# Sharing exponentials between ScalarE and VectorE: banks placed tile by tile, and two long passes in halves

## The chip, the cores and the metric

One core of a Trainium2 chip runs the whole program. The metric is device time of one execution in microseconds, lower is better. A core has five engines with a queue each: TensorE (PE, matmuls), ScalarE (ACT, activation functions), VectorE (DVE, element-wise work), GpSimd (POOL) and SyncE (SP, which here only issues DMAs). The queues run in order, and engines wait for one another by semaphores. PSUM, where matmuls write, has 8 banks of 512 float32 columns in each of 128 partitions.

## The reference

Four attention blocks with a residual, on 2048 tokens of width 640, 32 heads of width 20. Layers 0 and 2 look at a window of 256 keys, layers 1 and 3 at all keys.

```python
def _B_ref(x, wqkv, wo):            # layers 1 and 3; _A_ref (0 and 2) adds the window's mask
    qkv = (x @ wqkv).reshape(B, S, 3, H, Dh).transpose(2, 0, 3, 1, 4)
    q, k, v = qkv[0], qkv[1], qkv[2]
    scores = jnp.einsum("bhqd,bhkd->bhqk", q, k) * (Dh ** -0.5)
    p = _softmax(scores, axis=-1)
    o = jnp.einsum("bhqk,bhkd->bhqd", p, v)
    return o.transpose(0, 2, 1, 3).reshape(B, S, D) @ wo

x = x + _A_ref(_layernorm(x), A_wqkv, A_wo)
x = x + _B_ref(_layernorm(x), B_wqkv, B_wo)
x = x + _A_ref(_layernorm(x), A_wqkv, A_wo)
x = x + _B_ref(_layernorm(x), B_wqkv, B_wo)
```

## The kernel before

**Units, banks, tiles.** The kernel is one Python function that writes all queues by hand. Queries go in 4 chunks `c` of 512, heads in 8 groups `g` of four. A `Unit` is one layer, chunk and head group. Its work is a list of *banks*: for one block of 128 keys (`kc`, 16 of them) and one head `j`, the scores of 128 keys by 512 queries, which fill one PSUM bank; a full layer's unit has 64. Units stand in one list, `units`: layer 0, with parts of layer 1 chunk 0 woven in; the rest of layer 1 chunk 0; layer 1 chunks 1 to 3, with the window units of layer 2 between; layer 3 chunk 0 in two parts (key blocks 0 to 11, then 12 to 15), with layer 2's last chunk; layer 3 chunks 1 to 3. The main loop takes one *tile* per turn (a *tick*), as a rule three banks: three score matmuls into PSUM banks 0 to 2 or 3 to 5 by turns (L1359), one exponential by ScalarE over all three (L1387, 1536 columns to a bf16 tile `pt`), and some ticks later the matmuls with the values (L1420), which add into bank 7 (`op`).

**Background.** Projections, normalisations, transposes, output projections and the `tails` that end a unit are generators. `pump` and `keep_clock` run pieces of them between tiles; `keep_clock` also puts in matmuls that nobody reads (`unread`, or "owed" ones ahead of the next scores) when the tick has had too little TensorE work. Background results use PSUM bank 6 (`take_m`, `drop_m`), and VectorE empties it (L331, L579, L1128). All by-columns matmuls carry the line of their helper, L307.

**VectorE's exponentials.** Some banks of layers 1 and 3 are not given to ScalarE. VectorE computes their exponential in fixed point, for two banks at a time: a pass for each bank from PSUM to int32 (`side_fixed`, L957, 512 columns), then a chain over 1024 columns (`t_chain`): the fraction (L969) and its square (L978), the cubic (L980), and the whole part put in as the exponent (L982). The values matmuls of these banks are in `side_values` (L1010). Which banks they are is fixed when a `Unit` is made (`put_aside`): the last four (layer 1, chunks 1 to 3), the last six or eight in turn (layer 3 from chunk 1 group 1 on; four in the very last unit). None come from layer 1 chunk 0, layer 3 chunk 0 or the unit (3,1,0).

**Where they run.** Up to the final chunks (layer 3, chunks 1 to 3) the tiles are planned in a list ahead of the loop: a unit that gives banks gives them to its own tiles, 5 tiles apart, and such a tile has two banks for ScalarE (1024 columns) and one for VectorE, which reads it in place. In the final chunks tiles are full, and VectorE's score goes by itself into bank 6 (`side_scores`, L944), when the planner's count of VectorE's backlog, `state["lag"]`, is below `LAG` and no background piece holds the bank. The count rises with each VectorE instruction that is emitted (0.7 for a short pass, 1.2 for a long one) and falls by a tile's ScalarE time. `side_work` emits steps of the chain while it is below `WORK`, at the end of each tick. Working buffers: in layer 1 the float32 tile `raw_o`; from layer 3 chunk 1 on three tiles of `xnT`, with results in unused parts of `ka` and `qa` (`side_start`).

**Queues.** SP issues a unit's loads of queries, keys and values (L798, L810, L812) as soon as one of three key buffers is free; POOL issues the stores of projections and the loads of weights, and masks window banks (L1463).

Of the kernel before, what the change touches and what calls it, by code (L numbers as in the profile page):

```python
# [25 lines left out]
G = 8  # L26
# [14 lines left out]
WORK = 1.0  # L41
SIDE_1 = 4
SIDE_3 = (6, 8)
# [9 lines left out]
def kernel(  # L53
# [272 lines left out]
    def evac(out_, in_):  # L326
        if state["act"]:
            nc.scalar.copy(out=out_, in_=in_)
        else:
            state["lag"] += 0.6  # L330
            nc.vector.tensor_copy(out=out_, in_=in_)  # L331
# [60 lines left out]
    def stats(l, c, i):  # L392
        if (l, c) not in mvs:
            mvs[l, c] = lnp.tile([P, 4, 2], F32, name="mv", tag="mv")
        state["lag"] += 1.2
        st = lnp.tile([P, 2, 6], F32, name="stats", tag="stats")
        xv = x_sb[:, 4 * c + i, :]
        nc.vector.bn_stats(out=st[:, 0, :], in_=xv[:, 0:HD])
        nc.vector.bn_stats(out=st[:, 1, :], in_=xv[:, HD:D])
        nc.vector.bn_aggr(out=mvs[l, c][:, i, :], in_=st[:])  # L400
# [282 lines left out]
    def put_aside(l, c, g):  # L683

        if l == 1:
            n = SIDE_1
        else:
            n = 4 if (c, g) == (NC - 1, G - 1) else SIDE_3[g % 2]
        if n == 2:
            return ((NT - 1, 2), (NT - 1, 3))  # L690
        return tuple((NT - 1 - i // 4, i % 4) for i in range(n))

# [3 lines left out]
    class Unit:  # L696
        def __init__(self, l, c, g, part=None):
            self.l, self.c, self.g, self.part = l, c, g, part
            self.windowed = l % 2 == 0
            self.aside = ()  # L700
            if self.windowed:
                sets = [(m, b0, subs, j) for m, b0, subs in window_banks(c) for j in range(4)]
            else:

                if c > 0 and (l, c, g) != (3, 1, 0):
                    self.aside = put_aside(l, c, g)
                k0, k1 = key_blocks(l, part)
                sets = [
                    (None, 0, [(kc, 0, 4, 0)], j) for kc in range(k0, k1) for j in range(4)
                    if (kc, j) not in self.aside  # L710
                ]
            n = len(sets)
            self.banks = [
                (self, j, m, b0, subs, i < 4, i >= n - 4 + len(self.aside), i == n - 1)
                for i, (m, b0, subs, j) in enumerate(sets)
            ]
# [144 lines left out]
    def finish_unit(u):  # L861
# [31 lines left out]
    side_todo = deque(  # L893
        (u, p, i) for u in units for p in range(len(u.aside) // 2) for i in range(2)
    )
    side_left = Counter({id(u): len(u.aside) for u in units})
    side_out = {}
    side = {"xi": deque(), "chain": deque(), "out": deque(), "late": False}
# [7 lines left out]
    def side_start():  # L906

        assert live["xnT"] == 0 and not side["chain"] 
# [18 lines left out]
    def side_free():  # L927

        if not side_todo or not side["late"]:
            return False  # L930
        u, p, i = side_todo[0]
        return (
            id(u) in loaded and state["tick"] >= loaded[id(u)] + 8
            and mfree[6][0] <= state["tick"] and (i == 1 or len(side["xi"]) > 0)
        )

    def side_scores():

        u, p, i = side_todo[0]
        mseq[0] += 1  # L940
        mfree[6] = (state["tick"] + 2, mseq[0])
        kc, j = u.aside[2 * p + i]
# [4 lines left out]
    def side_fixed(z):  # L947

        u, p, i = side_todo.popleft()
        side_left[id(u)] -= 1  # L950
        if not side_left[id(u)] and id(u) in deferred:
            live["kt"] -= 1
            live["qt"] -= 1
        if i == 0:
            side["now"] = side["xi"].popleft()
        xi = side["now"]
        nc.vector.tensor_scalar(  # L957
# [4 lines left out]
        if i == 1:  # L962
            side["chain"].append(t_chain(u, xi))

    def t_chain(u, xi):

        V = nc.vector
        t = side["t"]
        V.tensor_scalar(  # L969
            out=t, in0=xi.bitcast(I16)[:, 0::2], scalar1=T1, scalar2=T0, op0=ALU.mult, op1=ALU.add  # L970
        )
        yield 0.7
        while not side["out"]:
            yield 0.0
        pt = side["out"].popleft()
        po = pt.rearrange("p a b -> p (a b)")
        q = po.bitcast(F16)
        V.tensor_tensor(out=q, in0=t, in1=t, op=ALU.mult)  # L978
        yield 0.7
        V.scalar_tensor_tensor(out=q, in0=q, scalar=TB, in1=t, op0=ALU.add, op1=ALU.mult)  # L980
        yield 1.2
        V.scalar_tensor_tensor(  # L982
            out=po.bitcast(U16), in0=xi.bitcast(I32), scalar=1.0 / C, in1=q,
            op0=ALU.mult, op1=ALU.add,
        )
        side["xi"].append(xi)
        side_out.setdefault(id(u), []).append((pt, state["tick"]))
        yield 1.2

    def side_work(force):  # L990

        while (force or state["lag"] < WORK) and side["chain"]:
            cost = next(side["chain"][0], None)
            if cost is None:
                side["chain"].popleft()
                continue
            if cost == 0.0:
                return False
# [5 lines left out]
    def side_values(u, pairs, done):  # L1004

        for n in range(done, len(pairs)):
            pt = pairs[n][0]
            for i in range(2):
                kc, j = u.aside[2 * n + i]
                nc.tensor.matmul(  # L1010
                    op[32 * j : 32 * j + VW, :], lhsT=u.v(kc, j), rhs=pt[:, i, :], start=False,
                    stop=all(jj != j for _, jj in u.aside[2 * n + i + 1 :]),
                    skip_group_check=True,
                )
            side["out"].append(pt)

    def side_push():
# [3 lines left out]
        if side_free():  # L1021
            side_scores()
            return
# [6 lines left out]
    def side_done(u):  # L1030

        n = 0
        while len(side_out.get(id(u), ())) < len(u.aside) // 2:
            n += 1
            assert n < 10000
            side_push()
        return side_out.pop(id(u))
# [5 lines left out]

    def s_emitted(u):
# [6 lines left out]
        elif side_left[id(u)]:  # L1051
# [187 lines left out]
    with tc.manual_schedule():  # L1239
# [11 lines left out]
        banks = [b for u in units for b in u.banks]  # L1251
        tiles = []
        starts = {}
        n = 0
        last_layer = sum(len(u.banks) for u in units[: index[3, 1, 0, None]])
        placed = {}
        while n < last_layer:
            size = 2 if len(tiles) % 2 and narrow(banks[n][0]) else 3
            u = banks[n][0]
            at = placed.setdefault(id(u), [])  # L1260
            extra = []
            if (
                len(at) < len(u.aside) and banks[n + 1][0] is u
                and len(tiles) >= (15 // (SIDE_1 - 1) if SIDE_1 > 2 else 3) * len(at) + (at or [0])[0]
            ):
                kc, j = u.aside[len(at)]
                extra = [(u, j, "side", 0, [(kc, 0, 4, 0)], False, False, False)]
                at.append(len(tiles))
                size = 2
            for b in banks[n : n + size]:  # L1270
                starts.setdefault(id(b[0]), len(tiles))
            tiles.append(banks[n : n + size] + extra)
            n += size
        for m, b in enumerate(banks[n:]):
            starts.setdefault(id(b[0]), len(tiles) + m // 3)
        banks = deque(banks[n:])

        side_now = False

        def next_tile(t):  # L1280

            if t < len(tiles):
                return tiles[t]
            size = 3
            if side_now:
                return [banks.popleft() for _ in range(min(size, len(banks)))]
            if t % 2 and not tails and state["held"] is None and mfree[6][0] < state["tick"]:
                if all(task.wake > state["tick"] for task in todo) :
                    size = 4
            return [banks.popleft() for _ in range(min(size, len(banks)))]  # L1290

        def rate(t):

            if t >= len(tiles):
                return 0.45
            u = tiles[t][0][0]
            if index[u.l, u.c, u.g, u.part] < woven:
                return 1.2
            done, r = 0.0, 0.6 if state["early"] else 0.3
            for task in todo:  # L1300
                done += max(task.left, 0.0)
                if task.need < len(units):
                    r = max(r, done / max(starts[id(units[task.need])] - t - 16, 1))
# [10 lines left out]
        last_tick[0] = len(tiles)  # L1314
# [4 lines left out]
        valued = 0  # L1319
# [4 lines left out]
        while ended is None or t < ended + 8:  # L1324
# [3 lines left out]
            if t < len(tiles) or banks:  # L1328
                if t >= len(tiles) and not side["late"] and not live["xnT"] and not todo:
                    side_start()  # L1330
                side_now = (
                    state["held"] is None and state["lag"] < LAG and side_free()
                )
                cur = next_tile(t)
# [28 lines left out]
                if cur[-1][2] == "side":  # L1363
                    cur = cur[:-1]
                    n_b -= 1
                    if "early" not in side:
                        side_early()
                    while not side_todo[0][2] and not side["xi"]:
                        assert side_work(True)
                    side_fixed(sp[:, n_b, :])  # L1370
                if side_now:
                    side_scores()
# [28 lines left out]
            for n in range(2 if n_b == 0 or t > closed + 1 else 0):  # L1401
# [15 lines left out]
                for m, (kc, q0, qn, col) in enumerate(subs):  # L1417
                    for _, pg, i, b in group:
# [4 lines left out]
                            start=(first and m == 0), stop=(last and m == len(subs) - 1),  # L1423
                            skip_group_check=u.windowed or len(u.aside) > 0,
                        )
                if first:
                    valued = 0
# [95 lines left out]
```

## Time and profile before

| | us |
|---|---|
| runs of the kernel (three): median, lowest, highest | 2191.64, 2187.83, 2196.76 |
| the profiled execution | 2197.81 |
| its span | 2196.1 |

The profiled execution falls into these stretches. A stretch begins with the first exponential of its first unit.

| stretch | us from the span's start | banks on VectorE |
|---|---|---|
| layer 0, with layer 1 chunk 0 woven in | 16 to 441 | 0 |
| layer 1 chunk 0, last key blocks | 441 to 497 | 0 |
| layer 1 chunk 1, with layer 2 | 497 to 753 | 32 |
| layer 1 chunk 2, with layer 2 | 753 to 1018 | 32 |
| layer 1 chunk 3, with layer 2 | 1018 to 1284 | 32 |
| layer 3 chunk 0, first part, with layer 2 | 1284 to 1500 | 0 |
| layer 3 chunk 0, second part | 1500 to 1558 | 0 |
| layer 3 chunks 1, 2, 3 | 1558 to 2182 | 56, 55, 47 |

How to read the lines: the page's busy line gives each engine's time, its share of the span and its instructions. A group of instructions has line, engine, operation, output and input with sizes, a count, then busy time in all and the mean of one in ns, then the engine's idle time just before them and what ended it. A line of waits says which engine at which line waited for which, how long in all in us, how often, and the longest. A line of stretches gives for each engine its busy time and instructions, then the granted clock of TensorE and the use of the DMA engines. Records of ScalarE's passes overlap their neighbours, so the distance between starts, not the mean length, is what a pass takes.

### The profile page before, as it was taken

Reading aid. Unit: us, or ns where it says so; the run is one execution under the profiler, and the core shown is the slowest. Engines: PE = TensorE matmul, PEld = TensorE weight load, DVE = VectorE, ACT = ScalarE, POOL = GpSimd, SP = SyncE. Lnnn points to the kernel's source line nnn. Section 1 sums busy time; section 2 is a strip of 40 time slices with the busy share of each in tenths; the row PEclk is TensorE's granted clock in tenths of the full one; section 3 lists DMA queues with packets and bytes.
Section 4 is the critical chain, followed back from the end, with each engine's and each line's share of the span. In section 5 each row is a group of like instructions: output and inputs, shape, how many; then the busy total and the mean of one; then the engine's idle time right before and its main releaser. Section 6 shows DMA issues by size and latency. Waiting matters only on the chain. (4 is left out here: it accounts for less than half of the span.)

```text
span 2196.1 us, 73000 instructions
## 1 busy us (share of the span) xinstructions
PE 1931.1 (88%) x31782; PEld 760.4 (35%) x31783; DVE 1324.3 (60%) x2308; ACT 2112.9 (96%) x1726; POOL 483.3 (22%) x952
## 2 busy tenths in 40 slices
PE   8999998988889888888888988888888988888887
PEld 3444443433333333333333433342222222222222
DVE  5556565425656666566665743532487778778873
ACT  7789899999999999999999999999999999999997
POOL 6665556110121113401143112511000000000000
PEclk9899999999999999999999999999999999999999
DMA  6223233322210323112231123122112111111100
GB/s 201 74 82 107 68 98 99 81 78 64 74 46 27 83 60 90 39 37 64 64 101 34 35 86 98 39 57 65 48 43 61 32 32 41 35 32 35 53 20 17
DMA packets 88416, 137.27 MB, mean 63 GB/s; under 512 B 20766, under 2 KB 63486, under 8 KB 88094
## 3 DMA queue, kind: packets, MB, share of 16 engines
q1 hardware_dynamic: 68878, 79.43, 13.1%
q0 software_dynamic: 19216, 53.17, 8.2%
q8 instruction: 249, 4.08, 0.8%
q14 instruction: 73, 0.60, 0.1%
HBM read 99.52 MB, written 27.79 MB: 58 GB/s over the span
## 5 line engine op out<-in xcount | busy, mean ns | idle before, releaser
L1387 ACT ACTIVATE pt<-ps 128x1536 bf16<-128x1536 f32 (+2 forms) x1646 | 2072.1, 1438 | 46.1 <-PE ps L1359 36.1
L1359 PE MATMUL ps<-qt,kt 32*128 32x512 bf16 x3938 | 542.4, 384 | 79.3 <-ACT pt L1387 70.2
L307 PE MATMUL ps<-masks,ident 128*32 128x512 bf16 x5676 | 504.6, 387 | 99.4 <-ACT pt L1387 54.8
L1420 PE MATMUL ps<-pt,vt 128*21 128x512 bf16 x3826 | 383.1, 387 | 1.1 <-issue 1.1
L1359 PEld LDWEIGHTS <-kt 32*128 32x128 bf16 x3938 | 161.0, 91 | 482.7 <-issue 461.0
L307 PEld LDWEIGHTS <-ident 128*32 128x32 bf16 x5676 | 179.9, 94 | 283.1 <-issue 254.7
L1463 POOL TENSOR_SCALAR_AFFINE_SELECT pt<-pt 128x256 bf16<-128x256 bf16 (+2 forms) x505 | 213.2, 444 | 184.4 <-ACT pt L1387 181.8
L307 PE MATMUL ps<-xnT,wqk 128*32 128x512 bf16 x3320 | 224.8, 381 | 12.4 <-DVE on L1128 2.8
L331 DVE CAST st<-ps 128x512 bf16<-128x512 f32 x134 | 92.7, 691 | 169.1 <-PE ps L307 164.9
L1420 PEld LDWEIGHTS <-vt 128*21 128x21 bf16 x3842 | 95.0, 89 | 254.9 <-issue 251.5
L957 DVE TENSOR_SCALAR xnT<-ps 128x512 int32<-128x512 f32 x158 | 109.2, 691 | 109.2 <-PE ps L944 108.4
L307 PE MATMUL ps<-wop,on 128*32 128x320 bf16 x3712 | 160.9, 300 | 6.8 <-DVE x_sb L579 3.3
L1474 DVE TENSOR_TENSOR pt<-pt,masks 128x512 bf16<-128x512 bf16 (+4 forms) x267 | 111.3, 433 | 61.3 <-ACT pt L1387 59.8
L307 PEld LDWEIGHTS <-on 128*32 128x32 bf16 x5760 | 122.2, 95 | 66.6 <-issue 33.6
L1359 PE MATMUL ps<-qa,ka 32*128 32x384 bf16 (+2 forms) x1408 | 114.5, 278 | 24.4 <-ACT pt L1387 21.2
L307 PE MATMUL ps<-wv,xnT 128*32 128x320 bf16 x2560 | 116.6, 302 | 7.9 <-DVE on L1128 3.3
L579 DVE TENSOR_TENSOR x_sb<-x_sb,ps 128x320 bf16<-128x320 bf16 x120 | 58.3, 486 | 105.8 <-PE ps L307 104.9
L307 PEld LDWEIGHTS <-wqk 128*32 128x32 bf16 x3320 | 83.5, 96 | 95.9 <-issue 38.0
L1128 DVE TENSOR_TENSOR on<-on,ps 128x512 bf16<-128x512 bf16 x128 | 86.3, 683 | 47.8 <-PE ps L307 46.9
L885 DVE CAST on<-ps 128x512 bf16<-128x512 f32 x112 | 77.1, 688 | 61.7 <-PE ps L1010 36.1
L957 DVE TENSOR_SCALAR raw_o<-ps 128x512 int32<-128x512 f32 x96 | 66.1, 689 | 61.4 <-PE ps L1359 60.3
L546 POOL DMA_DIRECT2D k_d<-st x75 | 42.6, 568 | 224.2 <-DVE st L331 209.1
(101 smaller groups left out, 1638.5 us busy)
## 6 DMA issues: line engine op xcount, KB each, us to landing
vt<-v_d SPq DMA_DIRECT2D x48, 336.0 KB
kt<-k_d SPq DMA_DIRECT2D x192, 80.0 KB
wqk<-in_B_wqkv_dram POOLq DMA_DIRECT2D x80, 160.0 KB, 3.5
wqk<-in_A_wqkv_dram POOLq DMA_DIRECT2D x70, 160.0 KB, 3.5
k_d<-st POOLq DMA_DIRECT2D x75, 128.0 KB, 2.3
q_d<-st POOLq DMA_DIRECT2D x75, 128.0 KB, 2.1
qt<-q_d SPq DMA_DIRECT2D x384, 20.0 KB
v_d<-vs POOLq DMA_DIRECT2D x16, 336.0 KB, 3.1
```

What stands on the lines that cost most here:

```text
L307: nc.tensor.matmul(out_[r], lhsT=lhsT[:, r], rhs=rhs, start=start, stop=stop)
L331: nc.vector.tensor_copy(out=out_, in_=in_)
L546: nc.gpsimd.dma_start(out=dst, in_=staging.pop())
L579: nc.vector.tensor_tensor(out=xv, in0=had, in1=yp, op=ALU.add)
L885: nc.vector.tensor_copy(out=oT, in_=op)
L957: nc.vector.tensor_scalar(out=xi.bitcast(I32)[:, i * C : (i + 1) * C], in0=z, scalar1=SCALE * LOG2E * FIX, scalar2=127.5 * FIX, op0=ALU.mu ...
L1128: nc.vector.tensor_tensor(out=oT, in0=oT, in1=zb, op=ALU.mult)
L1359: nc.tensor.matmul(sp[:, i, col * P : (col + qn) * P], lhsT=u.k(kc, j), rhs=u.q(j, q0, qn), start=True, stop=True,)
L1387: nc.scalar.activation(out=pt[:, i:k, b0 * P :], in_=sp[:, i:k, b0 * P :], func=ACT.Exp, scale=SCALE,)
L1420: nc.tensor.matmul(op[32 * j : 32 * j + VW, q0 * P : (q0 + qn) * P], lhsT=u.v(kc, j), rhs=pg[:, i, col * P : (col + qn) * P], start=(first ...
L1463: nc.gpsimd.affine_select(out=v, in_=v, compare_op=ALU.is_gt if later else ALU.is_ge, fill=0.0, base=0, pattern=[[0, k - i], [-1 if later ...
L1474: nc.vector.tensor_tensor(out=pt_[:, i:k, cols], in0=pt_[:, i:k, cols], in1=mv_, op=ALU.mult)
```

## The change

The list of tiles made ahead is gone, and each tile is made when its turn comes (`take`, `next_tile`). A unit keeps its banks in a queue, `rest`; tiles take from the front, and VectorE's banks are taken two at a time from the back (`side_take`), from a unit that `side_giver` finds: among the next three units whose loads were issued 8 ticks before, with at least 30 banks left in its queue (or 12 after its first pair). It gives none while the backlog count is not below 0.5, no working buffer is free or, before the final chunks' buffers are set up, the last bank was less than five tiles ago. All units of layers 1 and 3 but those of layer 1 chunk 0 may give, layer 3 chunk 0 among them, whose buffers are now set up (`side_start`) during its fourth head group or later, once at most one `xnT` is live and no window unit is.

A step of the chain is now emitted if the count with the step's own cost stays under a limit (2.2 in layer 3, 1.4 in layer 1), where the old test was the count alone, under 1.0. In layer 1 the two long passes run as two halves of 512 columns each. `side_values` emits the values of all pairs that are ready. Costs in the planner's count change (evacuations 0.7 or 0.5, statistics 1.1).

```diff
-WORK = 1.0
-SIDE_1 = 4
-SIDE_3 = (6, 8)
+LAG_1 = 0.5
+WORK = 2.2
+WORK_1 = 1.4
+KEEP = 30
+HALF = True
+MOST_1 = 64
+GAP_1 = 5
...
-    def side_free():
...
+    def side_giver():
+
+        if not side["late"] and state["tick"] < side["last"] + GAP_1:
+            return None
+        if side["half"] is not None:
+            return side["half"][0]
+        if not side["xi"]:
+            return None
+        while side["at"] < len(givers) and not givers[side["at"]].rest:
+            side["at"] += 1
+        for n in range(side["at"], min(side["at"] + 3, len(givers))):
+            u = givers[n]
+            if id(u) not in loaded or state["tick"] < loaded[id(u)] + 8:
+                return None
+            if not side["late" if u.l == 3 else "early"]:
+                return None
+            if u.l == 1 and len(u.aside) >= MOST_1:
+                continue
+            if len(u.rest) >= (KEEP if len(u.rest) + len(u.aside) < u.size else 12):
+                side["at"] = n
+                return u
+        return None
...
+        every = (slice(0, 2 * C),)
+        halves = (slice(0, C), slice(C, 2 * C)) if HALF and u.l == 1 else every
+        cost = 0.7 if len(halves) == 2 else 1.25
+        steps = [(fraction, h, 0.7) for h in every] + [(square, h, 0.7) for h in every]
+        steps += [(cubic, h, cost) for h in halves] + [(whole, h, cost) for h in halves]
+        return deque(steps)
...
     def side_work(force):
...
-        while (force or state["lag"] < WORK) and side["chain"]:
-            cost = next(side["chain"][0], None)
...
+            if not force and state["lag"] + cost > (WORK if side["late"] else WORK_1):
+                return False
...
+                giver = side_giver() if state["lag"] < (LAG if side["late"] else LAG_1) else None
+                if giver is not None and state["unit"] >= final and (
+                    state["held"] is not None or mfree[6][0] > state["tick"]
+                ):
+                    giver = None
+                cur = next_tile(t, giver)
```

## The prediction

> **What bounds the kernel now.** I read the busy shares of the page first:
>
> ```profile
> PE 1931.1 (88%) x31782; PEld 760.4 (35%) x31783; DVE 1324.3 (60%) x2308; ACT 2112.9 (96%) x1726; POOL 483.3 (22%) x952
> ```
>
> ScalarE (ACT) is busy for 96% of the span, and nearly all of it is the exponential of L1387. Then the busy times of stretches cut at the stage borders: layer 1 chunk 2, layer 3 chunk 0 (its first key blocks), layer 3 chunks 1 to 3.
>
> ```profile
> core 0: us, PE busy (x) PEld busy (x) DVE busy (x) ACT busy (x) POOL busy (x), PEclk, DMA share, GB/s
> 753.00:1018.00 265.00, 231.00 (x3877) 95.04 (x3870) 166.76 (x292) 261.56 (x205) 62.49 (x119) 0.99 0.23 62
> 1284.00:1500.00 216.00, 187.53 (x3255) 78.95 (x3245) 81.02 (x172) 214.92 (x161) 63.34 (x118) 1.00 0.24 67
> 1558.00:2180.00 622.00, 550.45 (x7287) 172.46 (x7284) 461.20 (x607) 617.89 (x457) 0.00 (x0) 1.00 0.12 36
> ```
>
> ScalarE is busy 99% of each stretch, VectorE (DVE) 63%, 38% and 74%. So from 441 us on the end is set by the columns ScalarE must pass, and VectorE has room, most of it from 1284 to 1558 us, where it takes no banks today. Next the groups by line with shapes kept apart, from 753 to 1284 us:
>
> ```profile
> L1387 ACT ACTIVATE pt<-ps 128x1536 bf16<-128x1536 f32 x342 | 473.1, 1535 | 9.3 <-PE ps L1359 8.7
> L1387 ACT ACTIVATE pt<-ps 128x1024 bf16<-128x1024 f32 x64 | 71.2, 1113 | 0.0
> ```
>
> The 64 narrow passes are the tiles that gave a bank to VectorE. The means, 1.535 and 1.113 us, overlap the neighbouring passes, so I price by starts: in the timeline unhindered passes of 1536 columns start 1.331 us apart, of 1024 columns 0.904 us. **A bank is worth 0.427 us, a pass costs 0.05 us beside its columns.** What the starts take beyond these prices is lost time: 28.1 us in layer 1 chunks 1 to 3 (497 to 1284 us, 624 passes, 96 banks on VectorE), 4.1 us from 1284 to 1558 us (203 passes, none on VectorE), 13.6 us from there to the last pass (158 banks). The idle column shows less, since a pass's record covers some of its wait.
>
> The waits tell whose slack is left. TensorE's (PE) own, 1558 to 2180 us:
>
> ```profile
> PE ps L307 <- ACT pt L1387: 40.5, 108, 0.9
> PE ps L944 <- DVE on L1128: 6.8, 19, 0.7
> PE ps L944 <- DVE x_sb L579: 5.2, 18, 0.6
> PE ps L1359 <- ACT pt L1387: 4.4, 15, 0.6
> ```
>
> Mostly TensorE waits for ScalarE (about 47 us here with a row of 2.2; the same query gives 80 us from 497 to 1558 us), and some 13 us for VectorE to empty the bank at L944.
>
> **The banks.** The order of the changed program, built but not run, has 302 fixed-point passes of VectorE where the old one has 254. Per stage: layer 1 chunks 1 to 3, 32+32+32 become 36+38+38 (+16); layer 3 chunk 0, none becomes 16+8 (+24); layer 3 chunks 1 to 3, 56+55+47 become 57+57+52 (+8). ScalarE's exponentials fall from 1650 to 1645 and lose 24,576 columns, 48 banks. 48 x 0.427 + 5 x 0.05 = **20.7 us less on the engine that sets the end.**
>
> **What a bank costs beside that.** A tile that gives a bank leaves ScalarE after 0.904 us, while TensorE still has three score matmuls, the values and a background block to do. Before, such passes took 0.08, 0.12 and 0.14 us over 0.904 on average in chunks 1 to 3, so 0.11. Bounds for the 40 banks up to 1558 us: 0.05, about what the late tiles with a bank lose over those without, and 0.16, which is 28.1 us less the quiet stretch's rate (4.1 / 203 x 624 = 12.6) over 96 banks. I take 40 x 0.11 = **4.4 us** (2.0 to 6.4). The late 8 go at 13.6 / 158 = 0.086: **0.7 us** (0.4 to 1.0).
>
> **VectorE's work.** From the groups with shapes kept apart:
>
> ```profile
> L957 DVE TENSOR_SCALAR raw_o<-ps 128x512 int32<-128x512 f32 x96 | 66.1, 689 | 61.4 <-PE ps L1359 60.3
> L980 DVE SCALAR_TENSOR_TENSOR raw_o<-raw_o 128x1024 f16<-128x1024 f16 x48 | 58.5, 1220 | 0.9
> L982 DVE SCALAR_TENSOR_TENSOR raw_o<-raw_o 128x1024 uint16<-128x1024 int32 x48 | 58.6, 1221 | 0.9
> L969 DVE TENSOR_SCALAR raw_o<-raw_o 128x1024 f16<-128x1024 int16 x48 | 33.2, 691 | 0.8
> ```
>
> 48 banks add 48 x 0.69 and 24 chains of two short passes (0.69 each) and two long ones (1.22 each): 33 + 92 = 125 us. The halves of layer 1 turn 112 long passes into 224. Half of one lies between 0.61 (no fixed part) and 0.69 us (a 512-column pass like L957), so the halves add 0 to 18 us; I take the upper end, nearest in shape. [...] All this lies beside ScalarE: by stage VectorE goes from 62% to about 70% (493 + 61 of 787 us), 35% to 58% (96 + 62 of 274 us) and 74% to 78% (461 + 21 of 622 us). Had it no room, the 143 us would be in the end.
>
> What reaches the path is lateness. In layer 1 a pass started ahead of an evacuation blocks it for up to 0.69 us instead of 1.22, and a tile gives a bank only while the planner's backlog is under 0.5 us, where places were fixed before. Waits of TensorE on VectorE there are some 32 us in the same view of 497 to 1284 us, most of it under its waits for ScalarE. I take **0**, between a gain of 5 us (a sixth of those waits) and a loss of 2 (more, smaller passes). In layer 3 chunks 1 to 3 passes may start on a higher planned backlog (limit 1.0 before a step, now 2.2 after it; the same ceiling for a long pass, more often reached). The planner's own count at the end of a tile rises there from 0.25 to 0.42 us on average, as the two programs are built. Against VectorE's lateness in proportion, 13.6 x 0.7 = 9.5 us is the worst; 0 the best, as TensorE's 47 us of waits for ScalarE cover it. I take **1 us**, since the longest wait on VectorE at L944 is 0.7 us in 622.
>
> **TensorE, DMAs, the end.** The matmuls are the same but for 20 more warming ones; each bank's score and two value matmuls only move. TensorE has 127 us of waits for ScalarE to give, of which 20.7 go. SP and POOL issue as many DMAs as before (1482 and 958 instructions on their queues). One load comes nearer to its use: layer 3 chunk 0 group 3, second part, is issued 4 tiles ahead instead of 8, 5.3 us. Its nine issues took 1517.7 to 1521.1 us before, 3.4 us, and POOL's DMAs land 2.1 to 3.5 us after issue: 0.2 to 1.6 us late. I take **0.5 us** once; what is queued behind it is one tile of scores. At the end one background projection finishes a tile later, but the last two value matmuls of VectorE's banks come earlier: **0** (-0.5 to +1).
>
> **Sum:** -20.7 + 4.4 + 0.7 + 0 + 1 + 0.5 + 0 = -14.1 us on a span of 2196.1 us: 2182.0. That execution took 2197.81 us, 0.3% over the median of the runs, 2191.64. From the median: **2177.5 us**. The bounds add to -23.6 and +0.8: 2168 to 2192.
>
> **Rivals.**
>
> *TensorE becomes the bound in the narrow tiles.* The gain of 0.427 us needs TensorE to follow in 0.904 us. Of the old narrow tiles, 67 that shared their tick with a background block lost 0.153 us, 29 without one 0.016. If the blocks crowd (3 score, 4 value and 20 projection matmuls in one tick were seen at 1248 us, with 0.64 us lost), the 40 banks cost 0.3 us each: 12 instead of 4.4, time 2185. Against it: 127 us of slack.
>
> *VectorE's lateness falls.* If halves and placing by backlog remove 5 us of layer 1's loss and layer 3's growing backlog stays covered: about -21, 2171 or lower.
>
> *Slower: a long pass put ahead of a bank's fixed-point pass in layer 3 chunks 1 to 3.* TensorE's next background matmul or side score into bank 6 waits for VectorE, and the values and scores behind it in TensorE's queue wait too. Price of one collision: 1.22 us less the 0.38 us that TensorE has at a mean wait on ScalarE (40.5 / 108), 0.84 us. It decides from 17 collisions (14.1 / 0.84), one in ten of 166 banks. At one in three, 55 x 0.84 = 46 us: 2177.5 + 46 = 2224. For it: the higher limit. Against it: 37 waits of 0.3 us in the old run for 158 banks, none over 0.7, and no higher ceiling.
>
> That the change gives VectorE no more banks is excluded by the built order.
>
> **How the numbers follow.** Forecast (2171 to 2183) 0.63; lateness falls 0.10; TensorE bound 0.18; slower 0.09. Half a percent, 11 us, is about what a measurement of this kernel can tell from no change (its three runs spread over 9 us). Faster than 2180.7: the second case and most of the first, 0.68. Slower than 2202.6: 0.07 of the last case. The rest, 0.25, is the same. The range takes the bounds above and 2 us at the low end and 1 at the high for the spread of the runs: 2166 to 2193.
>
> **What would show it.** The ScalarE group of 1024 columns near x276 and that of 1536 near x1284; the stretch that was 1284 to 1558 us about 8 us shorter, the layer 1 chunks together some 5 us, the last stretch about 2 us; VectorE near 1467 us busy, with passes of 512 columns at 0.61 to 0.69 us from the two halved lines; lost time from 441 us on near 52 us, where it was 46. Wrong if narrow passes start over 1.2 us apart on average (TensorE bound), or if TensorE's waits on VectorE at the side scores exceed 25 us (backlog).

## The result, and the profile after

The changed kernel takes 2174.09 us (median of four runs, 2173.51 to 2177.99), the kernel before 2189.9 us beside it. The ratio is 0.992, 95% interval 0.9906 to 0.9935: 0.8% faster, by 15.8 us. A second series gave 2171.83 against 2190.75 us, 0.9914 (0.9901 to 0.9927). The profiled execution took 2173.51 us, its span 2171.8.

The page's busy line, and ScalarE's groups with shapes kept apart:

```profile
PE 1927.8 (89%) x31803; PEld 753.7 (35%) x31803; DVE 1443.6 (66%) x2564; ACT 2095.1 (96%) x1721; POOL 490.6 (23%) x952
```

```profile
L1429 ACT ACTIVATE pt<-ps 128x1536 bf16<-128x1536 f32 x1284 | 1774.9, 1530 | 36.9 <-PE ps L1405 23.4 <-POOL pt L1500 3.1 <-PE ps L1462 2.2
L1429 ACT ACTIVATE pt<-ps 128x1024 bf16<-128x1024 f32 x276 | 295.1, 1072 | 7.4 <-PE ps L1405 6.7
```

ScalarE still sets the end at 96%, with 37 full passes fewer and 31 narrow ones more; VectorE is busy 119 us longer (1324.3 before). VectorE's own groups:

```profile
L981 DVE TENSOR_SCALAR xnT<-ps 128x512 int32<-128x512 f32 x190 | 131.0, 690 | 114.6 <-PE ps L964 108.7 <-PE ps L1405 4.1
L981 DVE TENSOR_SCALAR raw_o<-ps 128x512 int32<-128x512 f32 x112 | 76.9, 686 | 37.9 <-PE ps L1405 36.7
L1009 DVE SCALAR_TENSOR_TENSOR raw_o<-raw_o 128x512 f16<-128x512 f16 x112 | 74.2, 685 | 1.0
L1015 DVE SCALAR_TENSOR_TENSOR raw_o<-raw_o 128x512 uint16<-128x512 int32 x112 | 74.1, 684 | 0.0
```

190 + 112 banks are there, and the record of a half is 0.685 us, more than half of 1.22. But VectorE's records overlap their neighbours too. Where one pass follows another at once, starts lie 0.60 us apart after a half and 1.14 us after a whole pass (a timeline further down has such a pair: a record of 0.69 us starts at 1448.55, the next at 1449.16). So two halves take only some 0.06 us more than a whole one, at most 7 us for the 112; *nohalf_22* below, with as many banks and whole passes, has VectorE busy 4 us less, in layer 1 chunks 1 to 3 alone 7 us (530.65 against 537.83). The same overlap is why the records add up to 143 us more than before, while VectorE is busy 119 us more. By stretches (layer 1 chunks 1 to 3, layer 3 chunk 0, layer 3 chunks 1 to 3; the engines stand in the order PE, PEld, DVE, ACT, POOL):

```profile
490.00:1269.00 779.00, 691.14 (x11573) 280.68 (x11570) 537.83 (x1027) 768.70 (x623) 179.69 (x323) 1.00 0.22 60
1269.00:1540.00 271.00, 237.52 (x3992) 95.85 (x3991) 149.67 (x273) 265.16 (x205) 67.00 (x123) 1.00 0.25 67
1540.00:2157.00 617.00, 547.24 (x7279) 169.11 (x7273) 480.52 (x630) 613.05 (x453) 0.00 (x0) 1.00 0.13 36
```

The first two took 787 and 274 us before. From the start of the third to the last exponential it is 621 us, where it was 626. VectorE is now busy 69%, 55% and 78%.

**Where the profiles differ.** The two spans are 24.3 us apart, more than the medians. 6.9 us of this lie before the last key blocks of layer 1 chunk 0 (441 us in the kernel before), where the change does next to nothing. The kernel before, 50 to 120 us, and then the changed kernel:

```profile
50.00:120.00 70.00, 61.84 (x1398) 31.35 (x1402) 41.62 (x111) 54.05 (x72) 42.76 (x92) 0.90 0.26 73
```

```profile
50.00:120.00 70.00, 61.82 (x1493) 32.56 (x1485) 42.75 (x114) 56.79 (x76) 46.29 (x98) 0.98 0.30 81
```

The column after POOL's is TensorE's granted clock: 0.90 against 0.98, and TensorE, the busiest engine here, got through 95 matmuls fewer in the same busy time. That is one execution against another. From the first pass of the last key blocks of layer 1 chunk 0 to the last exponential it is 1743.1 against 1727.0 us: 20.7 less for columns and passes and 4.6 more lost between starts. The part after the last exponential is 1.2 us shorter.

### The profile page after: what moved, and what is told of

Its sections match the earlier page's. It is cut to its first block, busy times and chain, and to the rows that moved or that the text cites. A ratio compares the mean times of both kernels' runs of the same rounds, so it can differ in the third digit from the quotient of the medians.

```text
span 2171.8 us, 73321 instructions
## 1 busy us (share of the span) xinstructions
PE 1927.8 (89%) x31803; PEld 753.7 (35%) x31803; DVE 1443.6 (66%) x2564; ACT 2095.1 (96%) x1721; POOL 490.6 (23%) x952
## 5 line engine op out<-in xcount | busy, mean ns | idle before, releaser
L1462 PE MATMUL ps<-pt,vt 128*21 128x512 bf16 x3778 | 377.2, 386 | 0.5 <-ACT pt L1429 0.5
L1405 PEld LDWEIGHTS <-kt 32*128 32x128 bf16 x3930 | 156.2, 91 | 470.6 <-issue 452.1
L1500 POOL TENSOR_SCALAR_AFFINE_SELECT pt<-pt 128x256 bf16<-128x256 bf16 (+2 forms) x505 | 220.0, 458 | 189.4 <-ACT pt L1429 176.7
L311 PE MATMUL ps<-xnT,wqk 128*32 128x512 bf16 x3320 | 226.5, 382 | 10.5 <-DVE st L335 1.8
L981 DVE TENSOR_SCALAR xnT<-ps 128x512 int32<-128x512 f32 x190 | 131.0, 690 | 114.6 <-PE ps L964 108.7
L1462 PEld LDWEIGHTS <-vt 128*21 128x21 bf16 x3794 | 93.6, 89 | 252.8 <-issue 249.2
L1511 DVE TENSOR_TENSOR pt<-pt,masks 128x512 bf16<-128x512 bf16 (+3 forms) x267 | 113.9, 442 | 42.5 <-ACT pt L1429 41.1
L1405 PE MATMUL ps<-qa,ka 32*128 32x256 bf16 (+2 forms) x1408 | 116.9, 275 | 23.6 <-ACT pt L1429 18.9
L981 DVE TENSOR_SCALAR raw_o<-ps 128x512 int32<-128x512 f32 x112 | 76.9, 686 | 37.9 <-PE ps L1405 36.7
```

The costliest lines, as they stand in the source:

```text
L311: nc.tensor.matmul(out_[r], lhsT=lhsT[:, r], rhs=rhs, start=start, stop=stop)
L981: nc.vector.tensor_scalar(out=xi.bitcast(I32)[:, i * C : (i + 1) * C], in0=z, scalar1=SCALE * LOG2E * FIX, scalar2=127.5 * FIX, op0=ALU.mu ...
L1405: nc.tensor.matmul(sp[:, i, col * P : (col + qn) * P], lhsT=u.k(kc, j), rhs=u.q(j, q0, qn), start=True, stop=True,)
L1462: nc.tensor.matmul(op[32 * j : 32 * j + VW, q0 * P : (q0 + qn) * P], lhsT=u.v(kc, j), rhs=pg[:, i, col * P : (col + qn) * P], start=(first ...
L1500: nc.gpsimd.affine_select(out=v, in_=v, compare_op=ALU.is_gt if later else ALU.is_ge, fill=0.0, base=0, pattern=[[0, k - i], [-1 if later ...
L1511: nc.vector.tensor_tensor(out=pt_[:, i:k, cols], in0=pt_[:, i:k, cols], in1=mv_, op=ALU.mult)
```

## The experiments

Twelve kernels, in three groups, each measured beside the kernel before on one chip. "Lost" is the time by which ScalarE's passes start later than their width needs (1.331 us for 1536 columns, 0.904 for 1024), summed over layer 1 chunks 1 to 3, layer 3 chunk 0, and layer 3 chunks 1 to 3, in the profiled execution.

| kernel | us | ratio to before (95%) | banks in the three stretches | lost, us |
|---|---|---|---|---|
| before (profile) | 2190 to 2191 | | 96, 0, 158 | 28.1, 4.1, 13.6 |
| changed (profile) | 2174.1 | 0.992 (0.9906-0.9935) | 112, 24, 166 | 26.9, 10.6, 12.9 |
| again | 2171.8 | 0.9914 (0.9901-0.9927) | 112, 24, 166 | 25.0, 10.5, 11.6 |
| no30 | 2175.2 | 0.9924 (0.9913-0.9936) | 112, 0, 168 | 24.7, 2.6, 12.9 |
| nohalf | 2182.7 | 0.996 (0.9948-0.9973) | 110, 24, 166 | 34.4, 12.4, 11.7 |
| oldwork | 2172.0 | 0.9914 (0.9901-0.9927) | 114, 24, 166 | 24.6, 11.4, 12.2 |
| none | 2282.1 | 1.0414 (1.039-1.0438) | 0, 0, 0 | 11.1, 2.6, 11.5 |
| gap3 | 2181.8 | 0.9961 (0.9946-0.9975) | 136, 24, 166 | 45.2, 10.6, 11.4 |
| lag9 | 2230.1 | 1.0175 (1.0152-1.0198) | 112, 28, 198 | 25.2, 15.2, 74.9 |
| gap30 | 2174.4 | 0.9927 (0.9907-0.9946) | 112, 18, 166 | 24.8, 10.4, 11.4 |
| nohalf_22 | 2183.3 | 0.996 (0.9947-0.9974) | 112, 24, 166 | 36.9, 10.3, 11.6 |
| before_half | 2189.5 | 0.9989 (0.9979-0.9999) | 96, 0, 158 | 26.3, 3.8, 12.8 |
| gap3_22 | 2182.4 | 0.9963 (0.9949-0.9976) | 140, 24, 166 | 48.6, 10.5, 11.7 |
| gap4_22 | 2178.3 | 0.9939 (0.9928-0.9951) | 124, 24, 166 | 33.7, 10.5, 11.6 |

### The base, and what a bank is worth

*again* is the changed kernel itself.

> The changed kernel as it is, with the kernel before on the same chip, as the base for the other three. Both theories: 2174 us, 0.992 of the kernel before.

It held: 2171.8 us. *none* takes every bank from VectorE:

```diff
-    givers = [u for u in units if not u.windowed and (u.l, u.c) != (1, 0)]
+    givers = []
```

> VectorE takes no bank at all; all exponentials on ScalarE (302 banks back, price of columns and passes +130.5 us against the changed kernel). Theory (a bank is worth 0.427 us less about 0.08 us of lateness): slower than the changed kernel by 100 to 118 us, 2274 to 2292; lost time from 441 us on falls from 51 to between 20 and 35 us. Rival (TensorE is nearly the bound, a bank returns about 0.13 us): slower by only 40 to 60 us.

2282.1 us, 110 more than *again*: the theory. So 302 banks return 0.365 us each, of 0.427. Its stretches of layer 1 chunks 1 to 3 and layer 3 chunks 1 to 3:

```profile
497.00:1329.00 832.00, 702.88 (x11906) 296.40 (x11909) 265.43 (x592) 830.20 (x642) 176.74 (x329) 1.00 0.22 58
1608.00:2270.00 662.00, 528.28 (x7245) 173.67 (x7242) 56.01 (x121) 658.34 (x466) 0.00 (x0) 0.98 0.11 32
```

ScalarE (the fourth engine) fills both. Of the lost time 11 us stay in each, with no bank on VectorE: this part is not the banks' doing. The late stretch loses nearly the same with 166 banks as with none.

### Layer 3 chunk 0

*no30* takes no banks from layer 3 chunk 0:

```diff
-    givers = [u for u in units if not u.windowed and (u.l, u.c) != (1, 0)]
+    givers = [u for u in units if not u.windowed and (u.l, u.c) not in ((1, 0), (3, 0))]
```

> Layer 3 chunk 0 gives no banks (280 banks on VectorE instead of 302; the price of ScalarE's columns alone rises by 22 x 0.427 = 9.4 us). Theory (a bank is worth 0.427 us less some lateness): slower than the changed kernel by 3 to 8 us, about 2179; the lost time between the first unit of layer 3 and layer 3 chunk 1 falls from 10.6 to about 4 us. Rival (TensorE becomes the bound in narrow tiles, so that these banks return nothing): within 2 us of the changed kernel or faster.

3.4 us slower in the medians, at the low end of what the theory expected, with intervals that overlap: the rival's 2 us is not excluded. Lost time there falls by 7.9 us, which leaves 1.5 of the 9.4 us that the columns are worth. So these banks return some 0.07 (1.5 / 22) to 0.15 us (3.4 / 22) each. *gap30* spaces them five apart (the test on `GAP_1` then holds up to the final chunks):

> The spacing of five tiles holds in layer 3 chunk 0 too (12+6 banks there instead of 16+8, 296 in all; price +2.5 us). Theory (the banks there crowd: they stand two or three apart and lose 0.27 us each): within 2 us of the changed kernel, lost time there falling from 10.6 to under 8 us. Rival (spacing has no part in it): slower by 2 to 3 us, lost time unchanged.

Lost time hardly moved (10.4 us) with six banks fewer: crowding is not it, the rival holds as far as 2 us can be told. One place, the largest loss of the stretch (2.3 of 10.6 us), can be followed in the timeline of the changed kernel. VectorE, then TensorE, then ScalarE, near 1449 us (start, length; idle before in brackets):

```profile
1446.80 0.49 DVE L335 CAST vs<-ps 128x320 bf16<-128x320 f32 x1 [0.96 <-PE ps L311]
1447.20 1.22 DVE L1015 SCALAR_TENSOR_TENSOR qa<-xnT,qa 128x1024 uint16<-128x1024 int32 x1
1448.55 0.69 DVE L981 TENSOR_SCALAR xnT<-ps 128x512 int32<-128x512 f32 x1
1449.16 0.48 DVE L335 CAST vs<-ps 128x320 bf16<-128x320 f32 x1
```

```profile
1448.14 0.39 PE L1405 MATMUL ps<-qt,kt 32*128 32x512 bf16 x3
1448.47 0.39 PE L1055 MATMUL ps<-qa,vt 128*21 128x512 bf16 x2
1449.70 0.46 PE L311 MATMUL ps<-wv,xnT 128*32 128x320 bf16 x8 [0.84 <-DVE vs L335]
1450.09 0.39 PE L1405 MATMUL ps<-qt,kt 32*128 32x512 bf16 x3
```

```profile
1448.94 1.45 ACT L1429 ACTIVATE pt<-ps 128x1536 bf16<-128x1536 f32 x1 [0.75 <-PE ps L1055]
1451.74 5.05 ACT L1429 ACTIVATE pt<-ps 128x1536 bf16<-128x1536 f32 x4 [1.35 <-PE ps L1462]
```

The evacuation of `vs` stands behind a whole pass of 1.22 us and a bank's fixed-point pass, and starts at 1449.16. TensorE waits 0.84 us for the bank. The scores at 1450.09 stand behind that projection, and so do the value matmuls (L1462, from 1451.25) that, by the profile, release ScalarE's pass at 1451.74 after 1.35 us of idle time. The idle time before 1448.94 has another source: its scores began only at 1448.14, behind 20 matmuls of the projection before. Passes are whole here, since the halves are layer 1's alone. The stretch's other losses were not followed one by one, so that this is the cause of all of them is not shown.

### The halves

*nohalf* makes the long passes of layer 1 whole again:

```diff
-HALF = True
+HALF = False
```

> The two long passes of layer 1 whole again (300 banks; price of columns +0.8 us). Theory (VectorE has room, its shorter blocks hardly reach the end): 2173 to 2178, within 3 us of the changed kernel; lost time in layer 1 chunks 1 to 3 stays 25 to 29 us. Rival (halves are what takes the lateness away): 4 to 8 us slower, lost time there over 31 us. Second rival (halves cost VectorE 18 us that are in the end): faster by 3 us or more.

10.9 us slower: not the theory but the first rival, and more than its 8 us. Yet TensorE's waits for VectorE from 494 to 1279 us add to 32.6 us, hardly more than the changed kernel's 31.5. What stands out is the second line here, which the changed kernel has at 1.2 us.

```profile
PE ps L311 <- DVE st L335: 8.8, 20, 0.8
PE ps L1055 <- DVE raw_o L1015: 7.2, 6, 1.7
```

The values of VectorE's banks wait for the last pass of their chain. A whole pass counts 1.25 and rarely fits under the limit of 1.4, so chains might end after their unit. *nohalf_22* raises that limit (`WORK_1` 2.2 instead of 1.4), with whole passes:

> Whole long passes in layer 1 as in the run without halves, but the limit of the backlog count there is 2.2 instead of 1.4, so that a whole pass (1.25) is emitted sooner (302 banks; the planner holds a unit's last values back 7 times, 37 times in the run without halves, 17 in the changed kernel). Theory (what the halves bought is that a step fits under the limit, so that chains end before their unit does): 2172 to 2177, within 4 us of the changed kernel; TensorE's wait for the last pass at the values of VectorE's banks in layer 1 falls from 7.2 us to under 2. Rival (the length of a pass is what makes TensorE late): 2179 to 2185, as without halves.

2183.3 us. The waits at L1055 for VectorE are gone, but the time is as long as before: chains that end late are not all of it, and the rival's forecast holds. The waits are now others:

```profile
PE ps L311 <- DVE st L335: 11.3, 24, 1.1
PE ps L311 <- ACT pt L1429: 9.3, 28, 0.6
PE ps L311 <- DVE on L1175: 6.3, 15, 0.8
PE ps L311 <- DVE rts L1154: 5.2, 7, 1.5
```

Summed over that view, TensorE waits 38.4 us for VectorE, against 31.5 in the changed kernel. So whole passes cost time at both limits, with late chains at 1.4 and with other waits at 2.2. That the higher limit itself does harm to whole passes is not excluded, since halves with 2.2 at a spacing of five were not run. *before_half* puts halves alone into the kernel before:

```diff
-        V.scalar_tensor_tensor(out=q, in0=q, scalar=TB, in1=t, op0=ALU.add, op1=ALU.mult)
-        yield 1.2
+        for h in hs:
+            V.scalar_tensor_tensor(out=q[:, h], in0=q[:, h], scalar=TB, in1=t[:, h], op0=ALU.add, op1=ALU.mult)
+            yield 0.7 if u.l == 1 else 1.2
...
```

> The kernel before with nothing changed but the two long passes of layer 1 in halves (254 banks as before). Theory (halves by themselves do nothing): within 3 us of the kernel before. Rival (shorter passes make TensorE wait less): faster by 5 to 9 us. Second rival (15 us more of VectorE's time is in the end): slower by 5 us or more.

1.6 us faster: the theory, though the interval ends just under 1. Yet TensorE's waits for VectorE fell by as much, from 32 to 25 us. In the old placing TensorE waits 53 us for ScalarE in this stretch and in *nohalf_22* 43, so there is more room to take a late background matmul; that this is why the same 7 us gave 1.6 us there and 11 us here is argued, not shown.

The size of this difference needs care, since executions of one kernel differ with TensorE's granted clock: *nohalf_22* took 2183.93 to 2187.78 us at 0.992 or 0.993. At 0.998 or 0.999 *again* took 2170.49 to 2171.92 us, *nohalf* 2178.82, *nohalf_22* 2175.89 and 2176.19, *before_half* 2186.12 to 2186.48 and the kernel before beside it 2187.99 to 2189.24. At a like clock halves are thus worth 4 to 8 us here and 1.5 to 3 there. The rest of the 11 us came in executions at a lower clock. The last section shows a drop of the clock right behind a gap in TensorE's work, so whole passes may bring such drops about; that was not tested.

### The limit of the backlog

*oldwork* has the old test:

```diff
-            if not force and state["lag"] + cost > (WORK if side["late"] else WORK_1):
+            if not force and state["lag"] >= 1.0:
```

> A step of the chain is emitted under the old test, backlog count under 1.0, without its own cost (304 banks). Theory (the limit hardly matters, TensorE's waits for ScalarE cover the lateness): within 3 us of the changed kernel. Rival (the higher limit in layer 3 chunks 1 to 3 costs lateness): 3 us or more faster, with lost time there falling from 12.9 to under 10 us.

2172.0 against 2171.8: the theory. The late stretch lost 12.2 us, against 11.6 in *again* and 12.9 in the changed kernel's first profile, so the old limit saves nothing.

### More banks

*gap3* sets `GAP_1 = 3`.

> Tiles that give a bank in layer 1 may stand three apart instead of five (46+46+44 banks there instead of 36+38+38, 326 in all; price -10.2 us against the changed kernel). Theory: faster by 5 to 9 us, about 2167. Rival (narrow tiles so close make TensorE the bound or VectorE late): within 2 us or slower; lost time in layer 1 chunks 1 to 3 over 35 us instead of 27.

The rival: 10 us slower than *again*, and 20 us more lost for 24 banks, 0.84 us each. ScalarE's waits in layer 1, in *again* and then in *gap3*:

```profile
ACT pt L1429 <- PE ps L1405: 5.6, 19, 0.7
```

```profile
ACT pt L1429 <- PE ps L1405: 16.2, 41, 1.3
ACT pt L1429 <- PE ps L1462: 7.6, 5, 2.5
```

The second line of *gap3*, passes that wait for value matmuls to free their output, looked like chains that end late; so *gap3_22* and *gap4_22* raised `WORK_1` to 2.2 at spacings three and four.

> Spacing three instead of five in layer 1 with the limit at 2.2 instead of 1.4 (44+48+48 banks there, 330 in all; price of columns and passes -11.9 us against the changed kernel; 7 times held back, 31 with spacing three at limit 1.4). Theory (the 10 us that spacing three lost came from chains that ended after their unit): 2162 to 2170, faster than the changed kernel; ScalarE's waits for L1462 gone. Rival (more banks in layer 1 make VectorE or TensorE the bound): 2175 or more.

> Spacing four and limit 2.2 in layer 1 (40+42+42 banks there, 314 in all; price -5.0 us against the changed kernel; 7 times held back). Theory: 2166 to 2172. Rival: 2173 or more.

Neither is faster than the changed kernel. In *gap3_22* the second line is gone and the first has grown by as much, with four more banks:

```profile
ACT pt L1429 <- PE ps L1405: 24.0, 57, 1.7
ACT pt L1429 <- POOL pt L1500: 0.9, 2, 0.5
```

So at the higher limit the loss is scores that come late, and at both limits it grows faster than what a bank returns. TensorE still waits for ScalarE in *gap3* (43 us in all, 44 in *again*), and its waits for VectorE rise from 31 to 41 us; whether its own work or VectorE's lateness makes the scores late was not separated. *lag9* sets `LAG = 0.9`. Its output is wrong, for a reason that was not traced, so its time says only what this order of instructions takes.

> In layer 3 a bank may be given while the backlog count is under 0.9 instead of 0.5 (71+65+62 banks in chunks 1 to 3 instead of 57+57+52, 338 in all; price -15.9 us against the changed kernel). Theory (VectorE at 78 percent has room, 0.09 us lost per bank): faster by 8 to 13 us, about 2163. Rival (backlog: TensorE's side scores and background matmuls wait for VectorE, which would be over 90 percent busy): no faster, or slower, with TensorE's waits on VectorE at the side scores over 25 us instead of 12.

Slower by 58 us, but not as the rival had it. From 1530 to 2220 us VectorE was busy 564 us of 690, 82%, and TensorE's waits for VectorE at the side scores (L964) are 1.5 us. ScalarE's waits, then some of TensorE's:

```profile
ACT pt L1429 <- PE ps L1405: 65.5, 14, 25.5
```

```profile
PE ps L311 <- DVE on L1175: 10.2, 11, 2.2
PE ps L311 <- DMA wop<-in_B_wo_dram: 5.8, 1, 5.8
PE ps L311 <- DVE on L883: 5.6, 2, 5.4
PE ps L311 <- DMA on<-on: 4.6, 1, 4.6
```

14 waits make 65.5 us, one of them 25.5. TensorE waits inside output projections (`wop`, `on`) for a load of weights, for a DMA of `on` and for VectorE. Side scores and background share bank 6; that the former starved the latter until `finish_unit` had to force background work in one go fits these lines, and no run isolated it.

No kernel tried is clearly faster than the changed one. Halves in layer 3 chunk 0, which the timeline above suggests, were not tried.

## Why the prediction was right, and where it was not

2177.5 us was forecast, 2174.1 measured: -14.1 against -15.8 us.

- **ScalarE sets the end, a bank is worth 0.427 us: right.** The passes are x1284 and x276 as counted. Columns and passes make 20.7 us less, and 4.6 us more lost between starts leaves 16.1. *none* puts 110 us on 302 banks.
- **What a bank costs beside: near in the sum, by luck, and wrong by stretch.** 4.4, 0.7 and 1 us with 0.5 for the load make 6.6 more lost; 4.6 was measured. Layer 3 chunk 0 lost 6.5 us more than before, not 2.6 (24 banks at 0.27 instead of 0.11). Layer 1 lost 1.2 less than before, where 1.8 more was priced for its 16 banks, and the last stretch 0.7 less, where 1.7 more was priced. The three stretches are therefore 8, 3 and 5 us shorter, where 5, 8 and 2 were named as signs. The price of 0.11 came from layer 1 and was carried to a stage with whole passes and other background, the values projections among them. It was also read on narrow passes alone: of the 10.6 us in layer 3 chunk 0 these hold 3.9 us (0.16 each), and the full passes 6.8, where they held 4.1 before.
- **VectorE's lateness in layer 1, taken as 0 between -5 and +2: the step that failed.** Taking the halves away costs 10.9 us here, 4 to 8 at a like clock (*nohalf* and *nohalf_22*). What I left out is what 16 more banks would have lost with whole passes: 28.1 us became 34.4 (*nohalf*, 14 more banks) and 36.9 (*nohalf_22*). That is 6 to 9 us more, about all that the banks return, in profiled executions that took 3 to 5 us more than the medians of their kernels. The price of a bank was thus too low and the worth of the halves too low as well. Two errors of opposite sign made layer 1 come out near the forecast, which is luck.
- **VectorE's added work, 143 us beside ScalarE: right as a sum of records.** The records add up to 143 us more (1393.1 before, 1535.9 now). The record of a half is 0.685 us, near the upper end of the 0.61 to 0.69 us that the forecast put down for it. But VectorE is busy 1444 us, not near 1467: the prediction added records to a busy time, and records that follow at once overlap by 0.08 us. So the halves cost VectorE 4 to 7 us, not 18.
- **The higher limit in the last stretch, 1 us: nothing.** *oldwork* shows no difference. TensorE's waits on VectorE at the side scores rose from some 13 to 17 us, with 166 banks instead of 158, far from the 25 that would have spoken against the prediction, and the longest stayed at 0.7 us:

```profile
PE ps L311 <- ACT pt L1429: 39.1, 88, 0.9
PE ps L964 <- DVE on L1175: 9.1, 23, 0.7
PE ps L964 <- DVE x_sb L583: 6.9, 23, 0.7
```

- **The nearer load, 0.5 us: not seen;** TensorE's waits from 1265 to 1545 us hold no DMA of that unit. **The end, 0: -1.2 us.**
- **The rivals.** TensorE as the bound of narrow tiles did not come about. Beyond the change, at spacing three, each added bank loses 0.84 us, and whether TensorE or VectorE is behind that is open. The slower case did not come about at this limit; *lag9* is slower in another way. "Lateness falls" is half true: with whole passes it rose, and with halves it stayed level.

## What to carry to other kernels

A bank moved to an engine with room returned most of its columns on average (0.365 of 0.427 us), little in layer 3 chunk 0 (0.07 to 0.15 us), and less than nothing at spacing three (each added bank there lost 0.84 us). So price what the added work delays at the engine that feeds the bottleneck, here TensorE, not only whether the receiving engine has time. Where an engine serves both filler work and short urgent evacuations, the length of its longest instruction is a term of its own: here halving it gave 1.6 us in one order of the work and 11 in another. That the slack of the waiting engine decides between the two is argued, not shown. An average price per moved piece did not carry to another stage, nor beyond the count at which it was read. And where records of an engine overlap, as VectorE's do here by 0.08 us, add starts and not records.

## What was not expected of the hardware

TensorE was busy 88 and 89% of the span in the two kernels. Still its granted clock fell to 0.50 several times in every execution profiled: leaving *lag9* and the end after the last exponential aside, two times (*again*) to eleven (*none*), for 3.4, 6.8 or 10.2 us. Each of these drops came right behind 3.4 us in which TensorE was busy only 35 to 67% of the time (48 to 66% ahead of the four in the changed kernel). One of them in *nohalf* (after the length stands TensorE's busy time, and after the five engines its granted clock):

```profile
988.12:991.53 3.41, 1.42 (x20) 0.51 (x18) 2.80 (x4) 3.22 (x3) 0.00 (x0) 1.00 0.00 0
991.53:994.94 3.41, 3.36 (x36) 1.59 (x35) 1.18 (x2) 0.81 (x1) 0.00 (x0) 0.50 0.45 131
```

Other stretches as slack as these kept the full clock, six of 3.4 us at 61 to 66% in the changed kernel, so this is no rule. Some of the places differ between executions of the same instructions. *gap4_22* has the same program as the changed kernel up to VectorE's first bank: with 27.3 us at half clock until then it starts that pass (L981) at 496.89 us, the changed kernel with 6.8 us at 491.57. Such drops, 17 us of them before 441 us in the kernel before, are the likely reason why its profile is 6.9 us later there, so profiles are best compared stage by stage.
